# First gate's small operations on GpSimd, results in the place of low parts, a third bank for first products and a fifth split in the last segment

## The chip, the cores and the metric

The kernel runs on one core of a Trainium2 chip. Five engines work side by side, each on its own stream of instructions, and semaphores order them: TensorE (PE, matrix products), VectorE (DVE), ScalarE (ACT), GpSimd (POOL) and SyncE (SP, which issues transfers). The metric is the device time of one execution in microseconds. Three executions of the kernel before took 925.42, 928.76 and 929.61 us; the median is 928.76.

## The reference

Three stages, all in float32:

```python
# 1. attention within hash buckets: 2 batches, 8 heads, 768 positions, 64 dimensions, 6 sign bits
mask = q_bucket[:, :, :, None] == k_bucket[:, :, None, :]
scores = where(mask, q @ k.T / 8, -1e9);  attn = softmax(scores);  x = attn @ v   # -> 1536 x 512
# 2. mixture of 8 experts, noisy top 2
logits = x @ w_gate;  scale = log1p(exp(x @ w_noise));  noisy = logits + scale * noise
# the two largest of 8 per token, weights softmaxed over the two
for e in experts: out[tokens of e] += weight * (relu(x @ w1[e]) @ w2[e])           # 512 -> 1024 -> 512
# 3. second layer
h = x @ w_in;  out = (h - tanh(h)) @ w_out                                         # 512 -> 2048 -> 512
```

The inputs of the third stage come in float64 and are turned into float32 on the chip (`convert`).

## The kernel before, in words

*Products.* Every float32 operand is split into a high part (a copy in the format that PE takes at full rate) and a low part (the rest, a subtraction). A product is three PE passes: high by high, low by high, high by low. For weights, `split_w` makes both parts: ScalarE copies the high part (L851), then a subtraction makes the low part (L850): on GpSimd in two halves for the experts 0, 1 and 7, on DVE otherwise. Each weight tile holds two 128 x 512 blocks, one of the first matrix and one of the second. `fetch` brings the raw tile from memory into a buffer `wraw` of the pool `stg`, which has two of them; `next_w` fetches if needed and splits the next weight.

*Attention.* There are 16 heads in a row (2 batches of 8), 12 steps ("frames") a head, written out by hand in `plan`: `at_frame(t, f)` starts a generator at frame t, and each `yield` in it leaves the rest to the next frame. PE, DVE, ScalarE and SP take their instructions in this order. Per frame PE computes a block of scores for the row maximum (`smax`, L414, two banks of PSUM; DVE reduces it, L415) and a block for the exponential (`st_unit`, ScalarE L450, into one of five tiles p) and adds up p by v (`pv`). The sums of p over six blocks are five adds a head (`psum`, L483), on GpSimd or, where a bit of `PSV` is set, on DVE. GpSimd also has `vsum`, `nmterm`, the add in `evac` (L529) and the scatters.

*Gate.* Batch 0 is complete halfway through the heads, and its gate (`gate(0)`) runs beside the attention of batch 1, from frame 140 on: exponential on ScalarE, logarithm by three Newton steps, noise, top 2 by DVE's maximum and index search, one-hot `oh`, matrix `M`, prefix sums by PE (L709), positions `sidx`. The 128 tokens of a column of x then go by an indirect transfer on GpSimd's queue (`scatter`, L742) to their expert's rows in `Xg`. `gate(1)` runs after the attention, on DVE, with the first products of segment 0 as fill work for PE (`seg_fine`, `fill`): PE's order there is written by hand (`FILL`), and 30 of the 32 pieces stand before the first transposes of segment 1, whose rows `load_x(1)` reads from `Xg` once the scatters have landed. `gate_w` computes the two weights of each token, `results` the rows to gather later.

*Experts.* There are ten segments: expert 0 and expert 7 in two of 240 rows, one for each batch, the others with 448 rows. A segment has eight steps; a step is a first product (`h_step`, bank "b"), relu and its low part, and a second product (`y_step`, banks "c" and "d"). `y_out` copies the results from PSUM to SBUF, for the short segments into a `wraw` buffer, and `store` writes them to `Y`. `trans_x` transposes the next segment's rows (L1061) and makes their parts `xh` and `xl`. `LASTV` and `LASTW` list the steps of the last two segments in which another weight is split. At step 1 of segment 1 comes a branch (`overflow`) that all engines take part in.

*Second layer.* Four blocks of 384 rows with 16 steps each. `h2_step` computes the first product (bank "b", two banks), then tanh and a polynomial on ScalarE, DVE (L1379, L1381, L1383; the last of them frees the bank) and GpSimd (L1374), and the hidden rows' parts (L1394, L1399); `o2_step` the second product; `combine` transposes the rows of the next block, through bank "a".

Of the kernel before, what the change touches and what calls it, by code (L numbers as in the profile page):

```python
# [33 lines left out]
PSV = (0, 32, 32, 32, 32, 32, 32, 32, 32, 0, 0, 32, 0, 60, 32, 44)  # L34
# [9 lines left out]
LASTW = (2, 3, 5, 7)  # L44
# [32 lines left out]
def body(tc, q, k, v, proj, w_gate, w_noise, noise, w1, w2, w_in, w_out, out):  # L77
# [22 lines left out]
    with ExitStack() as ctx:  # L100
# [464 lines left out]
        def tables():  # L565
# [5 lines left out]
            nc.vector.tensor_tensor(spl, ends[:, 0], ends[:, 1], op=ALU.add)  # L571
            yield
            nc.vector.tensor_scalar(capv, spl, float(SEG - CAP), float(CAP), op0=ALU.mult, op1=ALU.add)
            b0 = basev[:, 0]
            nc.vector.tensor_scalar(b0, io8, float(CAP), float(B * SEG - CAP), op0=ALU.mult, op1=ALU.add)
# [45 lines left out]
        def gate(b):  # L621
            w = lambda name, shape, dt=F32: gx.tile(shape, dt, name=name)
            early = b < B - 1
            l3 = gd["lg", b].rearrange("p (c e) -> p c e", c=NC)
            y = w("g_y", [128, NC, E])
            nc.scalar.activation(y, l3[:, :, E:2 * E], AF.Exp)
            u = w("g_u", [128, NC, E])
            nc.vector.tensor_scalar(u, y, 1.0, None, op0=ALU.add)
            ln = w("g_ln", [128, NC, E])
            if b == B - 1:  # L630
                nc.scalar.activation(ln, u, AF.Ln)
            else:


                yield
                nc.vector.tensor_scalar(ln, u.bitcast(I32), LN2 * 2.0 ** -23, 0.0298 - 127 * LN2, op0=ALU.mult, op1=ALU.add)
                yield

            r = w("g_r", [128, NC, E])
            nc.vector.scalar_tensor_tensor(r, u, -1.0, y, op0=ALU.add, op1=ALU.subtract)  # L640
            if early:
                yield
            rc = w("g_rc", [128, NC, E])
            nc.vector.reciprocal(rc, u)
            if early:
                yield
            nc.vector.tensor_tensor(r, r, rc, op=ALU.mult)
            if early:
                yield
            nc.vector.tensor_tensor(r, r, nz[:, b], op=ALU.mult)  # L650
            if early:
                yield
            nc.vector.tensor_tensor(r, l3[:, :, 0:E], r, op=ALU.subtract)
            yield
            ei = w("g_ei", [128, NC, E])
            for _ in range(3 if b < B - 1 else 0):
# [6 lines left out]
                yield  # L663
                nc.vector.scalar_tensor_tensor(ln, ue, -1.0, ln, op0=ALU.add, op1=ALU.add)
                yield
            ny = w("g_ny", [128, NC, E])
            nc.vector.tensor_tensor(ny, ln, nz[:, b], op=ALU.mult)
            if early:
                yield
            nc.vector.tensor_tensor(ny, ny, r, op=ALU.add)  # L670
            yield
            v8 = w(f"g_v8{b}", [128, NC, 8])
            i8 = w("g_i8", [128, NC, 8], U32)
            for c in range(NC):
                nc.vector.max(out=v8[:, c], in_=ny[:, c])
# [8 lines left out]
            nc.vector.tensor_copy(e12, i8[:, :, 0:2].rearrange("p c t -> p t c"))  # L684
            yield
# [3 lines left out]
            if early:  # L689
# [3 lines left out]
                                    io8[:, None, None, :].to_broadcast([128, 2, NC, E]), op=ALU.is_equal)  # L693
            if early:
                yield
            nc.vector.tensor_tensor(M[:, b], oh[:, 0], oh[:, 1], op=ALU.add)
            yield
            if early:
                yield
# [20 lines left out]
            if early:  # L720
# [3 lines left out]
            else:  # L724
                pick(sidx[:, :, b], oh, ts)

        def pick(*a_):
            for _ in pick_steps(*a_):
                pass
# [800 lines left out]
```

## Time and profile before

| | us |
|---|---|
| median of three runs | 928.76 |
| the profiled execution: its own time | 933.93 |
| its span, first to last instruction | 932.1 |
| PE busy | 897.7 (96%) |
| DVE busy | 677.7 (73%) |
| ScalarE busy | 539.9 (58%) |
| GpSimd busy | 372.8 (40%) |

The profile is of one execution. Busy times are unions of an engine's instructions; an engine that isn't the slowest may stand idle at no cost. The idle time in front of an instruction is put down to what ended it. In the rows below, "L415" is line 415 of the kernel, and a tile's name stands without its buffer number.

### The profile page before, as it was taken

The page shows a single profiled execution, that of the slowest core. Times are in us where ns is not written, and L with a number is a line of the kernel's source. Part 1 is how long each engine was busy: PE and PEld are TensorE (multiplying, and loading weights), DVE is VectorE, ACT ScalarE, POOL GpSimd, SP SyncE. Part 2 cuts the span into 40 slices and gives each one's busy share as a digit, 9 for nine tenths or more (in the row PEclk, how much of TensorE's full clock was granted, in tenths as well). Part 3 has the DMA queues.
Part 4 walks back from the last instruction along what each step waited for, and adds up shares of the span by engine and source line. Part 5 has one row for each costly group of instructions (what it writes and reads, how often), then busy time and mean ns, then how long its engine had stood idle before and what let it go on. Part 6 is the DMA issues. An engine that isn't in the chain of part 4 may idle for free.

```text
span 932.1 us, 13632 instructions
## 1 busy us (share of the span) xinstructions
PE 897.7 (96%) x4736; PEld 699.3 (75%) x4736; DVE 677.7 (73%) x1290; ACT 539.9 (58%) x1039; POOL 372.8 (40%) x325
## 2 busy tenths in 40 slices
PE   8999999998997788999999999999999999999998
PEld 3555555554556677888888888888889899989997
DVE  7788787889757325797887878665888677677665
ACT  7658666864453133444444444454777777777765
POOL 6687778875667443000000004602342342342221
PEclk9999999999999899999999999999999999999999
DMA  5635553300222478686858777555420110110000
GB/s 123 171 117 170 159 182 106 103 24 7 93 64 95 163 222 256 218 287 214 271 199 292 236 255 248 174 197 179 135 69 1 57 46 1 57 46 1 35 1 34
DMA packets 104625, 123.72 MB, mean 133 GB/s; under 512 B 32121, under 2 KB 75177, under 8 KB 104553
## 3 DMA queue, kind: packets, MB, share of 16 engines
q1 hardware_dynamic: 100712, 110.23, 37.6%
q0 software_dynamic: 3840, 12.59, 4.0%
q8 instruction: 38, 0.62, 0.3%
q14 instruction: 35, 0.28, 0.1%
HBM read 82.79 MB, written 37.72 MB: 129 GB/s over the span
## 4 chain that ended last, share of the span: by engine, by line
PE 55%; DVE 3%; ACT 1%; DMA 1%; issue 1%; POOL 0%; DVEq 0%; SPq 0%; POOLq 0%
PE bank L1068 9%; PE bank L1070 9%; PE bank L1069 9%; PE bank L1095 8%; PE bank L1094 8%; PE bank L1093 8%; PE bank L1110 2%; PE bank L1061 1%; DVE g_u L1381 1%; PE bank L1350 1%; DMA xy<-Xg 1%; DVE wt L850 1%; DMA Y<-xy 0%; DVE hh L1399 0%; DVE g_u L1383 0%
## 5 line engine op out<-in xcount | busy, mean ns | idle before, releaser
L1068 PE MATMUL bank<-xh,wt 128*128 128x384 f32 (+2 forms) x544 | 186.3, 342 | 4.8 <-DVE g_u L1383 2.8
L1069 PE MATMUL bank<-xl,wt 128*128 128x384 f32 (+2 forms) x544 | 183.1, 337 | 0.0
L1070 PE MATMUL bank<-xh,wt 128*128 128x384 f32 (+2 forms) x544 | 183.1, 337 | 0.0
L1093 PE MATMUL bank<-wt,hh 128*128 128x512 f32 (+1 forms) x400 | 159.6, 399 | 9.5 <-ACT hh L1084 6.1
L850 POOL TENSOR_TENSOR wt<-wraw,wt 128x512 fp32r<-128x512 f32 x48 | 68.5, 1451 | 246.8 <-ACT wt L851 234.7
L1095 PE MATMUL bank<-wt,hh 128*128 128x512 f32 (+1 forms) x400 | 159.3, 398 | 0.1
L1094 PE MATMUL bank<-wt,hh 128*128 128x512 f32 (+1 forms) x400 | 158.9, 397 | 0.0
L1374 POOL TENSOR_TENSOR g_th<-g_h,g_th 128x384 f32<-128x384 f32 x64 | 67.2, 1050 | 187.2 <-ACT g_th L1373 186.7
L450 ACT ACTIVATE p<-bank 128x384 f32<-128x384 f32 x192 | 91.8, 489 | 72.1 <-PE bank L449 66.1
L415 DVE TENSOR_REDUCE mx<-bank 128x1 f32<-128x384 f32 x192 | 103.3, 551 | 31.1 <-PE bank L414 29.0
L1068 PEld LDWEIGHTS bank<-xh,wt 128*128 128x128 f32 x544 | 102.5, 188 | 13.9 <-DVE g_u L1383 4.8
L1069 PEld LDWEIGHTS bank<-xl,wt 128*128 128x128 f32 x544 | 102.5, 188 | 6.7 <-DVE xl L1353 0.2
L851 ACT ACTIVATE wt<-wraw 128x1024 fp32r<-128x1024 f32 x80 | 84.2, 1054 | 36.4 <-PE bank L1110 20.5
L1070 PEld LDWEIGHTS bank<-xh,wt 128*128 128x128 f32 x544 | 102.4, 188 | 3.1
L1093 PEld LDWEIGHTS bank<-wt,hh 128*128 128x128 f32 (+1 forms) x400 | 75.6, 189 | 22.9 <-ACT hh L1084 6.4
L483 POOL TENSOR_TENSOR ps<-ps,p 128x768 f32<-128x768 f32 x47 | 85.9, 1827 | 11.7 <-ACT p L450 7.1
L1095 PEld LDWEIGHTS bank<-wt,hh 128*128 128x128 f32 (+1 forms) x400 | 75.5, 189 | 18.3 <-DVE hh L1399 0.6
L1084 ACT ACTIVATE hh<-bank 128x448 fp32r<-128x448 f32 (+1 forms) x80 | 37.7, 473 | 83.6 <-PE bank L1070 34.9
L1086 DVE SCALAR_TENSOR_TENSOR hh<-bank,hh 128x384 fp32r<-128x384 f32 (+2 forms) x128 | 45.8, 388 | 54.7 <-ACT hh L1084 46.0
L1094 PEld LDWEIGHTS bank<-wt,hh 128*128 128x128 f32 (+1 forms) x400 | 75.5, 189 | 12.8
L474 PE MATMUL bank<-p,v 128*64 128x384 f32 x384 | 83.8, 515 | 0.0
L448 PE MATMUL bank<-qc,kb 108*128 108x384 f32 (+1 forms) x192 | 79.2, 412 | 1.8 <-DVE qc L438 1.6
(250 smaller groups left out, 1629.4 us busy)
## 6 DMA issues: line engine op xcount, KB each, us to landing
wraw<-in_moe_w_dram SPq DMA_DIRECT2D x128, 256.0 KB
cv_t<-in_moe_w_in_dram SPq DMA_DIRECT2D x16, 512.0 KB
cv_t<-in_moe_w_out_dram SPq DMA_DIRECT2D x16, 512.0 KB
W2f<-cv_w SPq DMA_DIRECT2D x16, 512.0 KB
wraw<-W2f SPq DMA_DIRECT2D x16, 512.0 KB
Xg<-zero SPq DMA_DIRECT2D x14, 512.0 KB
Y<-zero SPq DMA_DIRECT2D x9, 512.0 KB
xy<-Xg SPq DMA_DIRECT2D x6, 768.0 KB
```

The costliest lines, as they stand in the source:

```text
L415: nc.vector.tensor_reduce(MX[i % 2][:, c, hf:hf + 1], ps[:, :HF], op=ALU.max, axis=AX.X)
L448: nc.tensor.matmul(ps[:, :HF], KB[sn(g, par)][r, ck(kc)], QC[sn(g, par)][r, half(hf)], start=True, stop=False)
L450: nc.scalar.activation(hd["p", i, kc][:, half(hf)], ps[:, :HF], AF.Exp, scale=float(D) ** -0.5)
L474: nc.tensor.matmul(hd["o", i][hf * D:(hf + 1) * D, :HF], raw["v", g][:, par, kc], hd["p", i, kc][:, half(hf)], start=(kc == 0), stop=(kc = ...
L483: eng.tensor_tensor(t, hd["p", i, 0] if kc == 1 else t, hd["p", i, kc], op=ALU.add)
L851: nc.scalar.activation(t[:, 0], r, AF.Copy)
L1068: nc.tensor.matmul(ps[:, :n], ws(0, dc), xh[:, dc, :n], start=(dc == 0), stop=False)
L1069: nc.tensor.matmul(ps[:, :n], ws(0, dc), xl[:, dc, :n], start=False, stop=False)
L1070: nc.tensor.matmul(ps[:, :n], ws(1, dc), xh[:, dc, :n], start=False, stop=(dc == KD4 - 1))
L1093: nc.tensor.matmul(ps[:m], a, t[:, 0, 1], start=first, stop=False)
L1094: nc.tensor.matmul(ps[:m], a, t[:, 1, 1], start=False, stop=False)
L1095: nc.tensor.matmul(ps[:m], l, t[:, 0, 1], start=False, stop=last)
```

## The change

- `gate(0)` and `gate_w(0)`: sums, products, casts and copies move from DVE to GpSimd (`eng`); an operation that DVE does in one instruction with two steps becomes two on GpSimd. Reciprocals, maxima, index search, one-hot and everything that reads PSUM stay on DVE. At each hand-over the generator yields three more frames (`lead`). Both index columns are picked at once; the second half had been picked after attention. Head 10's last add of p moves from GpSimd to DVE (`PSV`). Three operations of `tables` move to GpSimd.
- The low parts of the two weights split beside `gate(1)` are kept back (`hd["lows"]`) until the gate's last step and are then made on DVE, in front of the scatters.
- `y_out` of short segments writes into the low-part tile `xl` of its own segment's rows, not into a `wraw` buffer.
- In the last segment a fifth weight is split (`LASTW`), and from its step 3 two raw weights may be fetched ahead. The transposes for the last segment come a step later.
- In the first block of the second layer, first products turn over three banks, until the next block's rows are transposed; until then "a" has one bank.

```diff
-PSV = (0, 32, 32, 32, 32, 32, 32, 32, 32, 0, 0, 32, 0, 60, 32, 44)
+PSV = (0, 32, 32, 32, 32, 32, 32, 32, 32, 0, 32, 32, 32, 60, 32, 44)
-LASTW = (2, 3, 5, 7)
+LASTW = (2, 3, 5, 6, 7)
...
         def gate(b):
...
+            eng = nc.gpsimd if early else nc.vector
+            lead = range(3 if early else 0)
...
+            eng.tensor_scalar(u, y, 1.0, None, op0=ALU.add)
...
+            if early:
+                eng.tensor_scalar(ln, u.bitcast(I32), LN2 * 2.0 ** -23, 0.0298 - 127 * LN2, op0=ALU.mult, op1=ALU.add)
...
+                eng.tensor_scalar(r, u, -1.0, None, op0=ALU.add)
+                eng.tensor_tensor(r, r, y, op=ALU.subtract)
+            for _ in lead:
+                yield
...
             nc.vector.reciprocal(rc, u)
...
+            eng.tensor_tensor(r, r, rc, op=ALU.mult)
+            eng.tensor_tensor(r, r, nz[:, b], op=ALU.mult)
+            eng.tensor_tensor(r, l3[:, :, 0:E], r, op=ALU.subtract)
...
+            for n in range(3 if early else 0):
+                if n:
+                    nc.scalar.activation(ei, ln, AF.Exp, scale=-0.5)
+                    yield
                 ue = w("g_ue", [128, NC, E])
-                nc.vector.tensor_tensor(ue, u, ei, op=ALU.mult)
-                yield
-                nc.vector.tensor_tensor(ue, ue, ei, op=ALU.mult)
-                yield
-                nc.vector.scalar_tensor_tensor(ln, ue, -1.0, ln, op0=ALU.add, op1=ALU.add)
-                yield
+                eng.tensor_tensor(ue, u, ei, op=ALU.mult)
+                eng.tensor_tensor(ue, ue, ei, op=ALU.mult)
+                eng.tensor_scalar(ue, ue, -1.0, None, op0=ALU.add)
+                eng.tensor_tensor(ln, ln, ue, op=ALU.add)
+                if n < 2:
+                    for _ in lead:
+                        yield
...
+            eng.tensor_copy(e12, i8[:, :, 0:2].rearrange("p c t -> p t c"))
...
+            eng.tensor_tensor(M[:, b], oh[:, 0], oh[:, 1], op=ALU.add)
...
-                gd["rest"] = (sidx[:, 1:2, b], oh[:, 1:2], ts)
-                yield from pick_steps(sidx[:, 0:1, b], oh[:, 0:1], ts)
+            for _ in pick(sidx[:, :, b], oh, ts, eng, lead):
+                yield
...
             nc.scalar.activation(t[:, 0], r, AF.Copy)
-            if key in (0, 1, E - 1):
+            if "lows" in hd:
+                hd["lows"].append(lambda: low(nc.vector, slice(0, 2)))
+            elif key in (0, 1, E - 1):
...
             if nb == 2:
-                yo = stg.tile([128, 2, DM], F32, name="wraw")
+                yo = mx[n % 2].tile([128, KD4, CAP], F32, name="xl")
+                yo = yo.rearrange("p c n -> p (c n)")[:, 0:2 * DM].rearrange("p (j d) -> p j d", j=2)
...
-        pick(*gd["rest"])
         run(scatter, 0, 1)
...
+        hd["lows"] = []
         next_w()
         gen = gate(B - 1)
...
+        for fn_ in hd.pop("lows"):
+            fn_()
         run(scatter, B - 1, 0)
         load_x(1)
...
-                while fn[0] < min(wn[0] + (PF if "st" in rings else 1), len(wsrc)):
+                while fn[0] < min(wn[0] + (PF if "st" in rings else 2 if last and f >= 3 else 1), len(wsrc)):
...
-                    if f == (5 + dc // 2 if n == B - 1 else 3 + dc):
+                    if f == (5 + dc // 2 if n == B - 1 else min(4 + dc, 6) if n == NSG - 2 else 3 + dc):
                         trans_x(n + 1, dc)
...
+        banks.update(a=[1], b=[2, 3, 0])
+        nbank["b"] %= 2
...
                 if f == 11 + j:
+                    if t0 == BC:
+                        banks.update(a=[0, 1], b=[2, 3])
+                        nbank.update(a=0, b=min(nbank["b"] % 3, 1))
                     combine(t0)
```

## Rows read from the trace of the kernel before

**Rows 1.** Windows by heads: length; busy us of each engine (instructions); PE clock; DMA

```profile
69.60:179.30 109.70, 109.70 (x643) 63.09 (x643) 88.07 (x188) 80.17 (x170) 85.67 (x71) 1.00 0.49 150
179.30:196.80 17.50, 17.40 (x103) 9.43 (x99) 14.48 (x34) 9.98 (x21) 14.92 (x12) 1.00 0.22 54
196.80:213.70 16.90, 16.19 (x93) 9.18 (x94) 16.31 (x36) 13.25 (x31) 12.64 (x13) 1.00 0.00 1
213.70:233.60 19.90, 16.92 (x92) 8.78 (x92) 19.61 (x54) 8.54 (x18) 10.75 (x7) 0.94 0.04 9
233.60:249.60 16.00, 15.79 (x81) 9.14 (x81) 11.53 (x30) 7.45 (x16) 11.37 (x9) 0.96 0.17 66
```

**Rows 2.** PE's waits over the span: us in total, times, longest

```profile
PE bank L1068 <- DVE g_u L1383: 2.8, 5, 1.0
...
PE bank L414 <- DVE mx L415: 1.8, 3, 1.4
```

**Rows 3.** Groups on DVE, 190 to 258 us: busy us, mean ns | idle before

```profile
L483 DVE TENSOR_TENSOR ps<-ps,p 128x768 f32<-128x768 f32 x5 | 4.7, 950 | 0.1
L662 DVE TENSOR_TENSOR g_ue<-g_ue,g_ei 128x48 f32<-128x48 f32 x3 | 4.0, 1322 | 0.0
...
L781 DVE TENSOR_TENSOR wAB<-g_f 128x6 f32<-128x6 f32 x1 | 0.8, 796 | 0.0
...
L628 DVE TENSOR_SCALAR g_u<-g_y 128x48 f32<-128x48 f32 x1 | 0.7, 657 | 0.1
...
L667 DVE TENSOR_TENSOR g_ny<-g_ln,nz 128x48 f32<-128x48 f32 x1 | 0.2, 199 | 0.0
```

**Rows 4.** Groups on GpSimd over the span

```profile
L483 POOL TENSOR_TENSOR ps<-ps,p 128x768 f32<-128x768 f32 x47 | 85.9, 1827 | 11.7 <-ACT p L450 7.1 <-DVE ps L483 2.2
...
L457 POOL TENSOR_TENSOR vs<-vs,v 128x128 f32<-128x128 f32 x32 | 14.6, 458 | 2.2
```

**Rows 5.** Timeline behind attention, several engines: start us, us, engine line; [idle before <- releaser]

```profile
293.18 4.96 POOL L850 TENSOR_TENSOR wt<-wraw,wt 128x512 fp32r<-128x512 f32 x4
...
294.40 3.78 DVE L684 CAST g_e<-g_i 128x12 f32<-128x12 uint32 x1 [0.71 <-DVE g_i L680]
...
299.05 0.20 PE L709 MATMUL bank<-M,before 128*128 128x48 bf16 x1 [4.31 <-DVE M L696]
...
301.19 0.99 POOL L742 DMA_INDIRECT Xg<-x,sidx  x1 [3.04 <-DVE tots L794]
...
310.38 0.41 SPq L1048 DMA_DIRECT2D xy<-Xg  x1
...
318.89 0.78 PE L1093 MATMUL bank<-wt,hh 128*120 128x512 f32 x1 [5.14 <-ACT hh L1084]
```

**Rows 6.** Timeline at the start of expert 1

```profile
356.35 0.52 ACT L1084 ACTIVATE hh<-bank 128x448 fp32r<-128x448 f32 x1
...
359.05 0.69 DVE L1125 COPY wraw<-bank 120x512 f32<-120x512 f32 x1 [1.45 <-POOL wt L850]
...
359.88 0.47 PE L1093 MATMUL bank<-wt,hh 128*128 128x512 f32 x1 [2.80 <-DVE wraw L1125]
```

**Rows 7.** Window behind that wait, columns as in rows 1

```profile
359.80:365.00 5.20, 5.12 (x16) 4.25 (x17) 4.25 (x6) 3.18 (x4) 3.27 (x2) 0.67 0.76 196
```

**Rows 8.** Timeline: the last segment's rows, issue and first use

```profile
612.77 0.35 SPq L1048 DMA_DIRECT2D xy<-Xg  x1
...
617.97 0.40 PE L1061 MATMUL bank<-ident,xy 120*128 120x120 f32 x2 [0.50 <-DMA xy<-Xg]
```

**Rows 9.** Timeline: the fifth wait for a bank, second layer

```profile
689.41 0.44 PE L1068 MATMUL bank<-xh,wt 128*128 128x384 f32 x1 [0.45 <-DVE g_u L1383]
```

**Rows 10.** Timeline: a scatter's issue beside DVE's add, and a low part on DVE

```profile
246.51 0.96 DVE L483 TENSOR_TENSOR ps<-ps,p 128x768 f32<-128x768 f32 x1
...
246.64 1.68 POOL L742 DMA_INDIRECT Xg<-x,sidx  x1 [0.17 <-issue]
...
365.96 1.21 DVE L850 TENSOR_TENSOR wt<-wraw,wt 128x1024 fp32r<-128x1024 f32 x1
```

More of the change, by code (lines that the diff above doesn't have):

```diff
@@ L570, in tables @@
             yield
-            nc.vector.tensor_tensor(spl, ends[:, 0], ends[:, 1], op=ALU.add)
+            nc.gpsimd.tensor_tensor(spl, ends[:, 0], ends[:, 1], op=ALU.add)
             yield
-            nc.vector.tensor_scalar(capv, spl, float(SEG - CAP), float(CAP), op0=ALU.mult, op1=ALU.add)
+            nc.gpsimd.tensor_scalar(capv, spl, float(SEG - CAP), float(CAP), op0=ALU.mult, op1=ALU.add)
             b0 = basev[:, 0]
-            nc.vector.tensor_scalar(b0, io8, float(CAP), float(B * SEG - CAP), op0=ALU.mult, op1=ALU.add)
+            nc.gpsimd.tensor_scalar(b0, io8, float(CAP), float(B * SEG - CAP), op0=ALU.mult, op1=ALU.add)
             yield
@@ L674, in gate @@
             for c in range(NC):
+                if early and c == NC // 2:
+                    yield
                 nc.vector.max(out=v8[:, c], in_=ny[:, c])
@@ L683, in gate @@
             e12 = w(f"g_e12{b}", [128, 2, NC])
-            nc.vector.tensor_copy(e12, i8[:, :, 0:2].rearrange("p c t -> p t c"))
-            yield
+            eng.tensor_copy(e12, i8[:, :, 0:2].rearrange("p c t -> p t c"))
+            if not early:
+                yield
+            else:
+                for _ in lead:
+                    yield
             AB = w("g_AB", [128, 2, NC])
@@ L692, in gate @@
             nc.vector.tensor_tensor(oh, AB[:, :, :, None].to_broadcast([128, 2, NC, E]),
-                                    io8[:, None, None, :].to_broadcast([128, 2, NC, E]), op=ALU.is_equal)
+                              io8[:, None, None, :].to_broadcast([128, 2, NC, E]), op=ALU.is_equal)
             if early:
                 yield
-            nc.vector.tensor_tensor(M[:, b], oh[:, 0], oh[:, 1], op=ALU.add)
+            eng.tensor_tensor(M[:, b], oh[:, 0], oh[:, 1], op=ALU.add)
             yield
-            if early:
+            for _ in lead:
                 yield
@@ L755, in gate_w @@
             v8, e12 = gd[b][3:]
+            early = b < B - 1
+            eng = nc.gpsimd if early else nc.vector
+            lead = range(3 if early else 0)
             dlt = w("g_d", [128, NC])
-            nc.vector.tensor_tensor(dlt, v8[:, :, 1], v8[:, :, 0], op=ALU.subtract)
+            eng.tensor_tensor(dlt, v8[:, :, 1], v8[:, :, 0], op=ALU.subtract)
+            for _ in lead:
+                yield
             nc.scalar.activation(dlt, dlt, AF.Exp)
-            if b < B - 1:
+            if early:
                 yield
@@ L762, in gate_w @@
             sm = w("g_sm", [128, NC])
-            nc.vector.tensor_scalar(sm, dlt, 1.0, 1e-9, op0=ALU.add, op1=ALU.add)
+            eng.tensor_scalar(sm, dlt, 1.0, 1e-9, op0=ALU.add, op1=ALU.add)
             yield
+            for _ in lead:
+                yield
             nc.vector.reciprocal(ws[:, 0], sm)
-            nc.vector.tensor_tensor(ws[:, 1], ws[:, 0], dlt, op=ALU.mult)
-            if b < B - 1:
+            if early:
                 yield
+            eng.tensor_tensor(ws[:, 1], ws[:, 0], dlt, op=ALU.mult)
             f = w("g_f", [128, 2, NC])
@@ L831, in results @@
                 yield
-                pick(yidx[:, :, b], oh, ty)
+                run(pick, yidx[:, :, b], oh, ty)
                 yield
```

83 lines of the change are left out of this document (34 added, 49 removed).

## Prediction

> **What bounds the kernel now.** I read the page's busy shares first: TensorE (PE) is busy for 96% of the span, so only the stretches where it stands, or where work comes to it slowly, can give time. The 40 slices show three such stretches, 190 to 250 us, 280 to 372 us and 605 to 700 us, and the two ends. I then asked for the stretches by window, for PE's idle rows, and for what the engine named there was doing.
>
> (a) Attention with the first gate beside it, 179 to 250 us. Seven heads at steady pace take 109.70 us, 15.67 each; the next four take 17.5, 16.9, 19.9 and 16.0, together 70.3, which is 7.6 more than 4 x 15.67 [rows 1]. In the third, VectorE (DVE) is busy for 19.61 of 19.90 us. The longest of PE's three waits for a row maximum on DVE is 1.4 us [rows 2]. The gate's operations make DVE late: one on 48 columns takes 0.20 us undisturbed, but the three of L662 took 1.32 on average, with GpSimd's 1.83 us adds beside them [rows 3, 4].
>
> (b) The second gate, after attention. GpSimd subtracts four low parts in 4.96 us from 293.18; DVE's cast of 12 columns, started at 294.40, takes 3.78 and ends with them, and PE stands 4.31 us until the gate's matrix M is there [rows 5].
>
> (c) The start of expert 1: PE stands 2.80 us for the copy of the segment's results, and that copy waited for GpSimd's low part, because results and raw weights share two buffers [rows 6]. The granted clock is 0.67 in the 5.2 us behind it [rows 7].
>
> (d) The last segment and the first steps of the second MoE: 0.50 us for the rows of the last segment [rows 8], and five waits on DVE's L1383, 2.8 us in all [rows 2], which means that the next first product has no bank. The last of them is 0.45 us [rows 9].
>
> **The change, part by part.** *First gate on GpSimd.* Thirty DVE operations between 191.55 and 256.6, 16.0 us by their own rows, leave DVE (first L628 0.66, last L781 0.80, thirty in all [rows 3]); 22 of them, 13.7 us, lie in the four heads. DVE's busy time there is 14.48 + 16.31 + 19.61 + 11.53 = 61.9 us [rows 1]; less 13.7, plus one 0.95 us add of head 10 that comes to DVE [rows 3], it is 49.2 in 62.7 us, 78%, against 80% at steady pace (88.07 of 109.70). So DVE stops being late. GpSimd gets 27 operations there and 8 behind, since it does a fused one as two. Their price is not in the trace on GpSimd: its add of 128 columns takes 0.458 us and of 768 columns 1.827 [rows 4], 2.14 ns a column, so 48 columns take 0.29 at the lower end and 0.46 at the upper; I take 0.36, nearer the lower since there are 48 columns. 27 x 0.36 = 9.7 us, less one add of 1.83: 49.7 becomes 57.6 of 62.7 us, 92%. That is more than its 78% at steady pace, and GpSimd takes work in order: behind a gate operation that waits for DVE or ScalarE stand the sums of p, which hold the five p buffers. So I take 4.5 of the 7.6 us; the ends are 7.6 and a loss, the rival below. The gate's 3-step spacing hides the hand-overs as long as GpSimd is under 4 us late. The rest of the old pick (second halves of the indices) leaves DVE at attention's end; PE's transposes end just before it, so nothing is taken for it, nor for the three table operations.
>
> *Low parts of two weights kept back.* With GpSimd's four subtractions gone from 293 us, the cast takes some 0.2 us like the gate's other small ones, M comes 3.6 us earlier and PE has its fill work until 294.8. The indices and scatters could then start 3.6 to 4.2 us earlier. But both subtractions now stand on DVE directly before the scatters, 2 x 1.21 us [rows 10], and a scatter issue on GpSimd took 1.68 us with a DVE add of two SBUF operands beside it, 0.99 elsewhere [rows 5, 10]. So the first scatter may lose up to 2.4 us. The load of the next segment is issued at 310.38 [rows 5]; such a load took 5.2 us to its use in the last segment (612.77 to 617.97 [rows 8]), so its rows are there at 315.6. PE without its unexplained 5.14 us wait would want them at about 315.2 (318.89 - 5.14 + 1.4 for one second product at full clock). Both move; the later one, the load, sets the gain: 1.8 to 4.2, I take 2.3. The low parts are wanted only at the eighth product and in the next segment, so their lateness is hidden by the fill; DVE's other low parts come up to 2.4 us later, which PE's slack before the load covers.
> The Trainium skill, page "SBUF — State Buffer", section "Who interferes with whom", has it that a tensor_tensor takes only the read interface shared with GpSimd, while descriptor generation needs the write one, and marks this as inferred. The 1.68 us row speaks against it; by the rule this part would give 4.2 us.
> The 5.14 us wait stays as it is in the sum: its row names ScalarE, but nothing on ScalarE explains it.
>
> *Results in the place of low parts.* The copy no longer waits for a weight's buffer: PE goes on at 357.1 in place of 359.88. What is late next are the first hidden rows of expert 1: ScalarE's relu starts at 356.35 and takes 0.52, then comes DVE's low part, some 0.7 like its copy of 512 columns [rows 6], so 357.6 for the block's third product, and PE waits up to 0.5. The low clock costs 0.33 x 5.2 = 1.7 us [rows 7] and goes with the wait. 2.8 + 1.7 - 0.5 = 4.0; lower end 1.0 (the weights' landing replaces the buffer), upper 4.5. The store reads the low-part buffer until it lands; the next writer of that buffer comes more than ten us later, so no new wait. With the buffers free, the weights' transfers start earlier too; I take nothing.
>
> *Third bank, fifth split, later transposes.* With three banks the first product waits for the step before; what is late next is the low part of the hidden rows (L1399), behind L1383 in DVE's order, for which the second product waits; of 0.45 us a step [rows 9] I take it to give 0.3 once, not in each, since DVE's pace is unchanged. DVE sets the pace in the five steps with a split (1.21 us of it on DVE [rows 10]); taken out of the fifth, it ends that a step sooner: the last wait, 0.45, and a lag of about 0.25 behind it, 0.7. In the last segment the split adds its 1.21 us on DVE ahead of the last block's transposed low part: 0.3 lost. The later transposes win the 0.50 us wait [rows 8] and give 0.2 back, since two now stand directly before the product that needs them. Together 1.0; the ends are -1.2 (the split in PE's way) and 3.3 (every wait gone).
>
> **Sum.** 4.5 + 2.3 + 4.0 + 1.0 = 11.8 us. The profiled execution took 933.93 us (span 932.1), so it would be 922.1; the runs' median of 928.76 is 5.2 lower, and less 11.8 it is **917.0 us**.
>
> **Rivals.**
> *GpSimd becomes the bound.* For: 92% at my price, and at 0.46 an operation 60.3 of 62.7 us before any wait for the lock. Against: head 13 gives it one add in place of four. The first term is then nothing: 917 + 4.5 = 921.5. The Trainium skill, "GPSIMD Engine Reference", section "4.1 Engine selection", is against elementwise work there too, with VectorE about twice as fast; the 1.83 us add beside DVE's 0.95 [rows 3, 4] agrees, and by twice 0.20 us an operation takes 0.40.
> *The weights' landing replaces the buffer* at expert 1: ScalarE's split ahead of the relu is fed by a transfer, and the queue is busy there (DMA share 0.76 [rows 7]). The third term is 1.0: 920.
> *The lows don't hold the scatters* (the page's rule above): the second term is 4.2, 915.1.
> *The gains are not kept:* the load of the second segment and the branch behind it are paced by transfers, so (a) and (b) come back as a wait there; only (c) and (d) stay, at half: 926.3.
> *Slower: GpSimd stands at the gate's hand-overs.* Seven times the gate goes from GpSimd to ScalarE or DVE and back. If GpSimd stands about 4 us each, with p's sums queued behind it, it needs 57.6 + 28 = 85.6 us where it had 70.3: 15.3 longer in place of 4.5 shorter, 917 + 4.5 + 15.3 = 936.8. It decides from 20 us of standing (57.6 + 12.7 + 7.3). For: GpSimd is in order. Against: the three steps kept free at each hand-over, about 4 us.
>
> **How the numbers follow.** Forecast 0.46, GpSimd the bound 0.15, weights 0.12, lows without effect 0.10, gains not kept 0.10, slower 0.07. About 0.5%, 4.6 us, is what a measurement of this kernel can tell from no change. Faster by more (under 924.1): 0.46 + 0.10 + most of 0.15 and 0.12, 0.81; within: 0.12; slower 0.07. The range runs from all upper ends together (7.6 + 4.2 + 4.5 + 3.3 = 19.6, so 909) to 926, nearly the case of gains not kept.
>
> **What would show it.** Right: the four heads at 16.5 us or less each and no L660 to L670 on DVE there; the cast behind the index search at 0.2 us and no 4.31 us wait; scatter issues stretched beside two DVE subtractions; no wait above 0.6 us at expert 1's first second-product and a full clock there; waits on L1383 gone, shorter ones on L1399 in their place. Wrong: GpSimd over 95% busy beside heads of 17 us and more; first products waiting for ScalarE's exponentials; a wait of several us for the second segment's rows.

## The result, and the profile after

The changed kernel took 915.24 us (median of four, 914.14 to 916.18), the kernel before 929.13 beside it (925.42 to 929.61). The ratio is 0.9855, with a 95% interval of 0.983 to 0.988: 13.5 us faster. I had said 917.0. A later session gave less: 919.14 (914.98 to 919.58) against 925.62, ratio 0.9906 (0.988 to 0.9932), 8.7 us. The ratios here and below go by all runs and are not quotients of the two medians, which would give 0.9930 and 6.5 us there. The sum came out close, in part by luck: its first term is not there on average, and the other three are together 3.2 us larger than I had said, as the rest of this text shows.

In the kernel after, lines have moved: first products are L1085 to L1087 (before L1068 to L1070), second products L1110 to L1112 (L1093 to L1095), the second segment's transposes L1078 (L1061), the low part of a weight L865 (L850), its high part L866 (L851), scatters L752 (L742), the gate's cast L694 (L684), the two last operations of the second layer's first products L1405 (L1383) and L1416/L1421 (L1394/L1399).

From the page of the changed kernel, its span, its busy times, and PE's row of 40 slices (each digit tenths):

```profile
span 912.1 us, 13613 instructions
PE 890.4 (98%) x4736; PEld 696.3 (76%) x4736; DVE 660.7 (72%) x1257; ACT 540.5 (59%) x1039; POOL 374.7 (41%) x357
...
PE   8999999999989899999999999999999999999998
```

PE went from 96% to 98%: of PE's busy time 7 us went, mostly half-clock stretches, and of its idle time 13. PE's waits after, largest first (line waited at, what ended it, us in total, times, longest):

```profile
PE bank L1078 <- DMA xy<-Xg: 3.5, 1, 3.5
PE bank L490 <- DVE ps L483: 3.0, 2, 2.4
PE bank L535 <- POOL x L529: 2.3, 1, 2.3
PE bank L1110 <- ACT hh L1416: 1.2, 4, 0.3
```

None of the waits that the prediction set out from [rows 2, 5, 6] is there any more; three new ones stand ahead. The heads of the first gate, in windows bounded like those of [rows 1] (length, then busy time of PE, its weight loads, DVE, ScalarE, GpSimd, then the granted clock, DMA share and GB/s):

```profile
179.00:196.10 17.10, 17.10 (x105) 9.37 (x99) 12.48 (x31) 9.85 (x21) 14.35 (x15) 1.00 0.23 56
196.10:213.90 17.80, 15.48 (x95) 8.93 (x93) 12.78 (x29) 13.27 (x30) 16.43 (x29) 1.00 0.00 1
213.90:230.00 16.10, 15.72 (x90) 8.77 (x87) 14.21 (x49) 8.43 (x18) 10.86 (x10) 1.00 0.06 11
230.00:245.10 15.10, 14.98 (x87) 8.73 (x86) 11.52 (x27) 7.67 (x17) 10.80 (x13) 1.00 0.13 52
245.10:259.40 14.30, 13.96 (x78) 7.39 (x78) 10.16 (x27) 7.27 (x16) 11.72 (x13) 1.00 0.77 256
259.40:273.60 14.20, 11.84 (x71) 6.64 (x70) 5.41 (x12) 7.74 (x19) 13.66 (x15) 1.00 0.11 37
```

The first four rows are the four heads of the sum, heads 10 to 13; they hold the same PE instructions as before and take 66.1 us in place of 70.3. In the second row GpSimd is busy for 16.43 of 17.80 us, and PE stands 2.3. The last row is head 15, where PE stands 2.4 us and GpSimd is busy for 13.66 of 14.20.

To compare more than one pair, I cut every profile at the same PE instructions: I from head 10's start to the end of attention (179.5 to 274.2 us before), II the second gate up to the first transpose of segment 1 (to 321.6), III the branch and the start of expert 1 (to 367.2), IV the last segment and the first steps of the second layer (610.6 to 700.0). The kernels are those of the next section; in brackets the time for which the granted clock was one half. The remaining stretches differ by at most 1.6 us between all kernels.

| kernel (profiled execution) | I | II | III | IV |
|---|---|---|---|---|
| before | 94.71 (3.4) | 47.39 (8.3) | 45.60 (5.4) | 89.35 |
| gate_alone | 93.95 (3.2) | 38.43 (0.9) | 44.38 (6.1) | 89.62 |
| lows_alone | 93.91 (0) | 37.49 (0) | 42.77 (3.4) | 89.98 |
| results_alone | 95.76 (6.8) | 40.76 (3.4) | 38.20 (0) | 89.75 |
| end_alone | 94.95 (3.4) | 41.11 (6.8) | 41.79 (3.4) | 88.35 |
| index_whole | 94.01 (0) | 40.80 (4.8) | 46.31 (5.5) | 89.69 |
| changed kernel | 92.46 (0) | 37.88 (1.3) | 39.45 (5.5) | 87.50 |
| after_again | 96.83 (10.1) | 38.89 (1.3) | 39.43 (5.6) | 87.50 |
| no_lows | 97.65 (10.2) | 42.22 (5.2) | 37.80 (1.6) | 87.45 |
| gatew_vec | 100.29 (13.7) | 38.93 (2.2) | 38.58 (1.2) | 88.12 |
| lows_late | 98.92 (13.7) | 38.53 (1.4) | 40.36 (5.4) | 87.72 |
| res0_raw | 93.98 (3.4) | 37.04 (0) | 41.01 (3.4) | 88.02 |
| no_bank | 96.75 (10.2) | 38.83 (0) | 38.45 (3.4) | 88.12 |
| best | 94.38 (6.8) | 37.98 (0) | 38.58 (3.4) | 87.74 |

### The profile page after: what moved, and what is told of

It is laid out like the page before. It is cut to its first block, busy times and chain, and to the rows that moved or that the text cites. A ratio compares the mean times of both kernels' runs of the same rounds, so it can differ in the third digit from the quotient of the medians.

```text
span 912.1 us, 13613 instructions
## 1 busy us (share of the span) xinstructions
PE 890.4 (98%) x4736; PEld 696.3 (76%) x4736; DVE 660.7 (72%) x1257; ACT 540.5 (59%) x1039; POOL 374.7 (41%) x357
## 4 chain that ended last, share of the span: by engine, by line
PE 61%; DVE 2%; ACT 1%; issue 0%; POOL 0%; DVEq 0%
PE bank L1085 10%; PE bank L1086 10%; PE bank L1087 10%; PE bank L1112 9%; PE bank L1111 9%; PE bank L1110 9%; PE bank L1127 2%; PE bank L1078 1%; DVE g_u L1403 1%; PE bank L1372 1%; DVE wt L865 0%; DVE g_u L1415 0%; DVE hh L1421 0%; DVE g_u L1405 0%; ACT hh L1416 0%
## 5 line engine op out<-in xcount | busy, mean ns | idle before, releaser
L1085 PE MATMUL bank<-xh,wt 128*128 128x384 f32 (+2 forms) x544 | 185.8, 342 | 0.1
L1087 PE MATMUL bank<-xh,wt 128*128 128x384 f32 (+2 forms) x544 | 183.3, 337 | 0.0
L865 POOL TENSOR_TENSOR wt<-wraw,wt 128x512 fp32r<-128x512 f32 x44 | 63.8, 1469 | 234.5 <-ACT wt L866 228.2
L1110 PE MATMUL bank<-wt,hh 128*128 128x512 f32 (+1 forms) x400 | 158.7, 397 | 1.2 <-ACT hh L1416 1.2
L1112 PE MATMUL bank<-wt,hh 128*128 128x512 f32 (+1 forms) x400 | 158.8, 397 | 0.7 <-DVE hh L1103 0.5
L1085 PEld LDWEIGHTS bank<-xh,wt 128*128 128x128 f32 x544 | 102.7, 189 | 7.2 <-ACTq L1279 0.6
L1087 PEld LDWEIGHTS bank<-xh,wt 128*128 128x128 f32 x544 | 102.5, 188 | 3.1
L866 ACT ACTIVATE wt<-wraw 128x1024 fp32r<-128x1024 f32 x80 | 84.3, 1055 | 24.5 <-PE bank L1127 20.4
L1112 PEld LDWEIGHTS bank<-wt,hh 128*128 128x128 f32 (+1 forms) x400 | 74.9, 187 | 19.7 <-DVE hh L1421 1.7
L1110 PEld LDWEIGHTS bank<-wt,hh 128*128 128x128 f32 (+1 forms) x400 | 75.0, 188 | 14.7 <-ACT hh L1416 2.4
L483 POOL TENSOR_TENSOR ps<-ps,p 128x768 f32<-128x768 f32 x45 | 82.3, 1828 | 4.9 <-DVE ps L483 2.2
L865 DVE TENSOR_TENSOR wt<-wraw,wt 128x1024 fp32r<-128x1024 f32 (+1 forms) x62 | 71.2, 1150 | 9.6 <-ACT wt L866 9.6
```

The costliest lines, as they stand in the source:

```text
L483: eng.tensor_tensor(t, hd["p", i, 0] if kc == 1 else t, hd["p", i, kc], op=ALU.add)
L865: low = lambda eng, h: eng.tensor_tensor(t[:, 1, h], r[:, h], t[:, 0, h].bitcast(F32), op=ALU.subtract)
L866: nc.scalar.activation(t[:, 0], r, AF.Copy)
L1085: nc.tensor.matmul(ps[:, :n], ws(0, dc), xh[:, dc, :n], start=(dc == 0), stop=False)
L1087: nc.tensor.matmul(ps[:, :n], ws(1, dc), xh[:, dc, :n], start=False, stop=(dc == KD4 - 1))
L1110: nc.tensor.matmul(ps[:m], a, t[:, 0, 1], start=first, stop=False)
```

## The experiments

Three sessions of four kernels, each session on another chip and beside the kernel before; no_bank ran only once.

| kernel | us | before | ratio, 95% interval |
|---|---|---|---|
| gate_alone | 923.73 | 927.81 | 0.9950, 0.9931 to 0.9970 |
| lows_alone | 922.83 | 927.81 | 0.9956, 0.9942 to 0.9970 |
| results_alone | 920.83 | 927.81 | 0.9927, 0.9907 to 0.9947 |
| end_alone | 925.30 | 927.81 | 0.9977, 0.9961 to 0.9994 |
| index_whole | 933.95 | 934.43 | 1.0000, 0.9981 to 1.0019 |
| no_lows | 921.76 | 934.43 | 0.9863, 0.9846 to 0.9881 |
| gatew_vec | 923.56 | 934.43 | 0.9888, 0.9869 to 0.9908 |
| lows_late | 921.86 | 934.43 | 0.9857, 0.9839 to 0.9875 |
| after_again | 919.14 | 925.62 | 0.9906, 0.9880 to 0.9932 |
| best | 915.39 | 925.62 | 0.9879, 0.9856 to 0.9903 |
| res0_raw | 918.50 | 925.62 | 0.9921, 0.9893 to 0.9950 |
| no_bank | 919.28 (one run) | 925.62 | none |

### Each part alone

The four parts of the diff, each put on the kernel before by itself.

> The kernel before with the first part alone: first gate's sums and products on GpSimd, with the three table operations, PSV[10] = 32 and the whole index pick in place of its two halves. Theory 1 (read from the two traces): the four heads win 4.7 us and head 15 gives 2.4 back, because the last weights' six small operations stand on GpSimd ahead of the sums of p; 2.3 to 2.5 us in all, so about 926.7 against 929.1. Theory 2 (my prediction's term): the 2.4 us lost in head 15 belong to the other parts, the gate alone is worth 4.5: 924.6. The trace decides by PE's wait at L490 in head 15.

> The kernel before with the second part alone: the low parts of two weights kept back past the second gate and taken on VectorE. Theory 1: it moves the matrix M, the scatters and the load of the second segment 4 us earlier and wins 2.7 us, 926.4; the 3 us that the changed kernel wins behind the branch (PE's 2.0 us there, 1.1 us at the next second product) are not here. Theory 2: these 3 us come with it, since everything is issued earlier: 5.7 us, 923.4. Prediction's term: 2.3.

> The kernel before with the third part alone: results of the four two-block segments written to the place of the low parts. Theory 1: the buffers of raw weights come free, so their transfers start before the second segment in place of behind its predecessor's store; the branch wait and the 1.1 us wait behind it go too: 4.65 + 3.0 = 7.7 us, 921.4. Theory 2: only the copy at the start of expert 1 is freed and the clock behind it: 4.65 us, 924.5 (prediction's term: 4.0, 925.1).

> The kernel before with the fourth part alone: third bank, fifth split, later transposes. Theory 1: 1.85 us, as the two traces differ behind 610 us: 927.3. Theory 2 (prediction's term): 1.0 us, 928.1. Nothing before 600 us is changed here, so its trace also shows again what the kernel before does at 318.89 us: if the 5.14 us wait there belonged to the one profiled execution alone, this trace has none over 1 us before that second product; if it belongs to the kernel, it is there again.

By the ratios they gain 4.6, 4.1, 6.8 and 2.1 us: 17.6 together, more than the 13.5 of the whole. Two of the parts must buy the same thing, and the traces say which. In gate_alone the low parts are still on GpSimd, and yet PE's wait for M, 4.31 us before [rows 5], is 1.2. Two of PE's waits in gate_alone (lines are those of each kernel; M's are L723 and L710 here):

```profile
PE bank L490 <- DVE ps L483: 3.0, 2, 2.4
...
PE bank L723 <- DVE M L710: 1.2, 1, 1.2
```

And the order of time there, GpSimd's rows from 287 us and DVE's cast (start, duration, line):

```profile
287.61 2.53 POOL L865 TENSOR_TENSOR wt<-wraw,wt 128x512 fp32r<-128x512 f32 x2 [2.81 <-ACT wt L866]
291.56 2.58 POOL L865 TENSOR_TENSOR wt<-wraw,wt 128x512 fp32r<-128x512 f32 x2 [1.42 <-ACT wt L866]
...
294.34 0.17 DVE L694 CAST g_e<-g_i 128x12 f32<-128x12 uint32 x1
```

The four low parts start at 287.61 and 291.56, not all at 293.18 [rows 5], and are over when the cast comes. In the kernel before six scatter issues stood ahead of them, those of the index half that was picked after attention. The order of time in the kernel before, first and last of the six:

```profile
285.77 1.01 POOL L742 DMA_INDIRECT Xg<-x,sidx  x1 [0.16 <-DVE x L527]
...
292.21 0.98 POOL L742 DMA_INDIRECT Xg<-x,sidx  x1 [0.30 <-issue]
```

With both halves picked at once these six move to 248 to 256 us, beside head 14. So theory 1 for gate_alone was right about head 15 (L490, 2.4 us) and missed this; theory 2's gain, 4.5 us, is near the measured one for another reason than it gave. lows_alone lies between its theories (4.1 us, 2.8 to 5.4); the wait for M is gone, and the wraw wait at expert 1 still there (2.0). results_alone went by theory 1: 6.8 us (4.9 to 8.6), where theory 1 said 7.7 and theory 2 4.65. end_alone's interval (0.6 to 3.6 us) holds both theories; in stretch IV it is 88.35 against a mean of 89.68 in the five profiles without this part, 1.3 us. It and results_alone leave the work from 300 to 320 us as it was, and PE stands for no more than 1.2 us there: the 5.14 us of [rows 5] don't belong to every execution (last section).

### The scatters alone, and the change without the low parts

```diff
# index_whole, on the kernel before
-                gd["rest"] = (sidx[:, 1:2, b], oh[:, 1:2], ts)
-                yield from pick_steps(sidx[:, 0:1, b], oh[:, 0:1], ts)
+                yield from pick_steps(sidx[:, :, b], oh, ts)
...
-        pick(*gd["rest"])
# no_lows, on the changed kernel: split_w, and the lines that open and empty the list
-            if "lows" in hd:
-                hd["lows"].append(lambda: low(nc.vector, slice(0, 2)))
-            elif key in (0, 1, E - 1):
+            if key in (0, 1, E - 1):
```

> The kernel before with one thing changed: both halves of the first gate's indices are taken at once, where the first half stood, and the second half at the end of attention is gone. Gate, adds and low parts stay where they were. Theory 1: in the kernel before six second scatters stand on GpSimd from 285.77 to 293.2 us, ahead of the four low parts; with the indices known early they are issued earlier, the low parts come earlier, and the 12-column cast and PE's 4.31 us wait go to about 1.2 us, as they did with the gate alone: 3 us faster, 924.8 against 927.8. Theory 2: the cast's wait is the low parts' own and goes only when they leave GpSimd: no change, 927.8, or slower by the larger index operations in head 13.

> The changed kernel without the lows kept back (they are on GpSimd again). Theory 1: the early scatters have already freed GpSimd, so PE's wait for M is 1.2 us in place of none, and the first scatter issue is 0.98 in place of 1.77 us: 0.4 us slower than the changed kernel, 915.6. Theory 2: the lows kept back are worth here what they were worth alone on the kernel before, 5.0 us: 920.2. My prediction's term for them: 2.3, 917.5.

PE's waits in index_whole, before the second product and for M:

```profile
PE bank L1092 <- issue: 4.3, 1, 4.3
...
PE bank L709 <- DVE M L696: 1.2, 1, 1.2
```

The cast there:

```profile
294.49 0.17 DVE L684 CAST g_e<-g_i 128x12 f32<-128x12 uint32 x1
```

At its place theory 1 holds to the digit: two lines of index code, with the gate still on DVE, take the cast to 0.17 us and the wait from 4.31 to 1.2. The time did not follow (933.95 against 934.43, 1.8 us to either side); its profile is of its fastest execution (927.84 of 927.84 to 938.73) and so can't say where the 3.1 us went in the others. That stays open; the last section names a loss in head 14, beside these scatters, that other kernels of the second session had and this profile has not. no_lows: 0.9863 beside 0.9857 for lows_late, the changed kernel with an edit without effect (below), in the same session. So the low parts kept back are worth 0.6 us with the scatters early, by intervals of 1.6 us to either side each: theory 1's 0.4 fits, the 5.0 that they bring alone does not. In stretch II no_lows does take 3.3 to 3.7 us more than gatew_vec and lows_late, but 2.1 of that is a longer standstill of the kind in the last section (5.5 us against 3.4) and 1.2 the wait for M, and its stretch III is shorter. What they cost shows in GpSimd's rows of no_lows:

```profile
295.41 2.58 POOL L865 TENSOR_TENSOR wt<-wraw,wt 128x512 fp32r<-128x512 f32 x2 [1.42 <-ACT wt L866]
301.37 1.01 POOL L752 DMA_INDIRECT Xg<-x,sidx  x1 [3.38 <-DVE tots L809]
```

Its first scatter issue takes 1.01 us where the changed kernel's takes 1.77 (next part).

### The lows behind the scatters

```diff
-        for fn_ in hd.pop("lows"):
-            fn_()
         run(scatter, B - 1, 0)
         load_x(1)
+        for fn_ in hd.pop("lows"):
+            fn_()
```

> The changed kernel with the two kept-back low parts taken behind the first six scatters and the load of the second segment, in place of ahead of them. Theory 1 (the row of the changed kernel): two subtractions on VectorE, 2.36 us from 293.89, hold the first scatter issue at 1.77 in place of 0.98 us; it comes back to 1.0, the scatters and the load are 0.8 us earlier, PE's 3.5 us wait for the load is 2.7: 0.8 us faster, 914.4. Theory 2 (the Trainium skill, page SBUF - State Buffer, section Who interferes with whom: a tensor_tensor leaves descriptor generation alone): the first issue stays at 1.7 us and the time at 915.2.

The edit moved nothing: DVE takes the two subtractions in its own order, right behind the indices, whatever GpSimd's program says. Its rows are those of the changed kernel, 6.9 us later. So it told nothing apart: with the subtractions still beside it, the first issue takes its 1.77 us by either theory. The changed kernel in order of time, DVE, GpSimd, SP's load and PE's first transpose of those rows:

```profile
291.06 0.17 DVE L694 CAST g_e<-g_i 128x12 f32<-128x12 uint32 x1
...
293.89 1.22 DVE L865 TENSOR_TENSOR wt<-wraw,wt 128x1024 fp32r<-128x1024 f32 x1
...
294.24 1.77 POOL L752 DMA_INDIRECT Xg<-x,sidx  x1 [11.10 <-DVE sidx L748]
296.31 0.98 POOL L752 DMA_INDIRECT Xg<-x,sidx  x1 [0.30 <-issue]
...
304.62 0.41 SPq L1065 DMA_DIRECT2D xy<-Xg  x1
...
309.61 0.63 PE L1078 MATMUL bank<-ident,xy 120*128 120x120 f32 x2 [3.46 <-DMA xy<-Xg]
```

What does tell it apart is the set of all 14 profiles: the first issue took 1.73 to 1.77 us in the eight with two such subtractions on DVE beside it, 0.99 to 1.01 in the six without. Page "SBUF — State Buffer" of the Trainium skill, section "Who interferes with whom", has it that a tensor_tensor leaves descriptor generation alone, an inference by its own words; here it does not. The price is 0.8 us, not the 2.4 of my bound: one issue is held for about as long as the first subtraction still had to run, 0.87 us; the next issue takes 0.98.

### The weight step of the first gate on VectorE

```diff
             early = b < B - 1
-            eng = nc.gpsimd if early else nc.vector
+            eng = nc.vector
```

> The changed kernel with the first gate's weight step (the nine small sums and products behind the indices) on VectorE again, the gate itself left on GpSimd. Theory 1: the 2.36 us for which PE stands at L490 in head 15 come from the six small operations and the hand-overs ahead of the sums of p on GpSimd; the wait goes: 2.4 us faster, 912.8. Theory 2: GpSimd is late there by its twelve scatter issues from 240 to 256 us, and the wait stays above 1.5 us: 914.5 or more.

The wait at L490 went (0.8 us in two, the longest 0.6), but so did it in lows_late and no_lows, in the same session, without this edit: there head 14 took 20.0 and 20.1 us, where it takes 14.0 in the changed kernel. Head 14 in no_lows and in the changed kernel:

```profile
247.30:267.40 20.10, 17.41 (x79) 8.44 (x79) 10.41 (x25) 6.87 (x15) 17.01 (x21) 0.83 0.57 195
...
245.40:259.40 14.00, 13.96 (x78) 7.39 (x78) 9.86 (x25) 6.98 (x15) 11.59 (x12) 1.00 0.78 261
```

PE stood in no_lows and lows_late three times for 0.8 to 0.95 us beside the scatters and then ran at half clock for 6.8 us, and GpSimd was no longer late. gatew_vec lost as much in that head (21.6 us). Its ratio, 0.9888, is the worst of the three, with intervals that overlap. Theory 1 is not shown: in the second session PE came too late to wait for GpSimd.

### Where the results go

```diff
             if nb == 2:
-                yo = mx[n % 2].tile([128, KD4, CAP], F32, name="xl")
...
+                if n == 0:
+                    yo = stg.tile([128, 2, DM], F32, name="wraw")
+                else:
+                    yo = mx[n % 2].tile([128, KD4, CAP], F32, name="xl")
```

> The changed kernel with the results of the first segment alone back in a buffer of raw weights, those of the second segment and of the last two still in the place of low parts. Theory 1: the transfers of the next weights wait for that segment's store again, PE's branch wait (2.0 us in the kernel before) and the 1.1 us at the second product behind it come back, and the start of expert 1 stays without its 2.8 us wait: 2 to 3 us slower than the changed kernel. Theory 2 (my prediction, which took nothing for earlier transfers): the whole gain hangs on the second segment's results, and this kernel takes as long as the changed one.

SP's rows and ScalarE's split in res0_raw:

```profile
306.07 0.39 SPq L893 DMA_DIRECT2D wraw<-in_moe_w_dram  x1
314.75 0.35 SPq L1148 DMA_DIRECT2D Y<-wraw  x1
315.15 1.74 SPq L895 DMA_DIRECT2D wraw<-in_moe_w_dram  x1
...
320.60 1.06 ACT L866 ACTIVATE wt<-wraw 128x1024 fp32r<-128x1024 f32 x1 [4.87 <-DMA wraw<-in_moe_w_dram]
```

The second half of a raw weight (L895) is issued at 315.15, behind the first segment's store; ScalarE then stands 4.87 us for it with the branch behind it, and PE at the branch, by its waits:

```profile
PE bank L1085 <- ACTq L1282: 2.5, 1, 2.5
```

The changed kernel's rows for the same:

```profile
295.60 0.51 SPq L895 DMA_DIRECT2D wraw<-in_moe_w_dram  x1
...
296.73 0.68 SPq L895 DMA_DIRECT2D wraw<-in_moe_w_dram  x1
...
318.75 1.06 ACT L866 ACTIVATE wt<-wraw 128x1024 fp32r<-128x1024 f32 x1 [1.03 <-PE bank L1112]
```

Two whole weights are fetched by 297 us, and ScalarE waits for PE, not for a transfer. Stretch III is 41.01 against a mean of 38.86 in the eight profiles with all results in the low parts' place: 2.2 us, theory 1 by its mechanism. What it is worth in all is less clear: stretch II is the shortest of all there (37.04), and over II and III together res0_raw takes 78.1 us where the changed kernel, after_again, no_bank and best take 76.6 to 78.3, 77.4 on average. By time the two kernels can't be told apart (0.9921 and 0.9906).

### The third bank

no_bank leaves out the two `banks.update` pieces of the change and keeps the fifth split and the later transposes.

> The changed kernel without the third bank for first products, the fifth split and the later transposes kept. Read from its trace between 610 and 700 us of the kernel before, where the changed kernel won 1.7 + 0.2 us. Theory 1 (prediction: 0.3 for the bank, 0.7 for the split): the five waits for VectorE's L1403, 2.8 us in all in the kernel before, are four or five again, and about 0.3 us is lost. Theory 2: the bank carries nearly all of it, since the first of these waits is 1.0 us: 1.3 us lost.

Four of the five waits for DVE are back (at L1405, which is L1383 before; the L1403 of the expectation is a slip), but stretch IV is 88.12 against a mean of 87.72 in the seven profiles with the whole part (87.45 to 88.12): 0.4 us, no more than those differ among themselves. That is theory 1, the prediction's 0.3, and not theory 2; with the bank, waits of 1.2 us on L1416 stand in the place of these 2.3. PE's wait in no_bank:

```profile
PE bank L1085 <- DVE g_u L1405: 2.3, 4, 1.0
```

### The changed kernel again, and a better one

best is the changed kernel with four edits: the two of the parts before (weight step, lows), and

```diff
-... 32, 32, 32, 60, 32, 44)
+... 32, 32, 32, 60, 48, 44)
...
-            (nc.vector if i >= NI - 1 else nc.gpsimd).tensor_tensor(xs, xs, hd["t", i], op=ALU.add)
+            (nc.vector if i >= NI - 1 or i == 9 else nc.gpsimd).tensor_tensor(xs, xs, hd["t", i], op=ALU.add)
```

> The changed kernel once more, on the chip of the three runs beside it, as their base. Its ratio was 0.9855 (0.983 to 0.988). Theory: its two waits in attention (2.3 us at L535, 2.4 at L490) and the 3.5 us before the second segment are there again; the half-clock stretches may lie elsewhere, since in ten profiles they followed all eleven PE waits of over 3 us, but only eight of fourteen between 2 and 3. Rival: the waits themselves differ from chip to chip, and then a comparison of single traces tells little.

> The changed kernel with GpSimd relieved at the two places where PE waited for it: the x add of head 9 on VectorE (2.3 us wait at L535), one more sum of head 14 on VectorE (PSV[14] = 48) and the weight step of the first gate on VectorE (2.4 us at L490); and the kept-back low parts behind the first six scatters (0.8). Theory 1: the three waits go to 0.9, 0 and 2.7: 4.6 us faster than the changed kernel, ratio to before 0.9805. Theory 2: VectorE becomes late in heads 11 to 14 as it was before the change, waits for row maxima come back, and nothing is left: 0.9855.

after_again has the first profile's waits in attention again, by PE's waits:

```profile
PE bank L490 <- DVE ps L483: 3.0, 2, 2.4
PE bank L535 <- POOL x L529: 2.3, 1, 2.3
```

And yet stretch I is 4.4 us longer and II 1.0. Windows of after_again at and behind those two waits (columns as in [rows 1]; behind GpSimd the granted clock, the DMA share and GB/s):

```profile
204.00:208.00 4.00, 1.68 (x14) 0.95 (x10) 1.40 (x4) 2.27 (x7) 3.67 (x8) 1.00 0.00 0
208.10:211.30 3.20, 3.20 (x13) 2.19 (x10) 0.96 (x3) 0.62 (x3) 2.79 (x7) 0.50 0.00 0
...
269.60:276.20 6.60, 6.17 (x24) 3.64 (x25) 1.10 (x3) 1.82 (x6) 5.29 (x4) 0.50 0.25 78
```

Here the clock went to 1.2 GHz (0.50 in the row) behind both waits, for 3.4 and 6.8 us, with PE busy; in the first profile it did so behind neither. PE's list of waits in attention is otherwise the same.

best: 914.97 to 915.47 in five runs, after_again 914.98 to 919.58 in six. The medians differ by 3.75 us, but the intervals of the ratios overlap: probably better, not shown to be. The waits at L535 and L490 are gone (0.6 left of the latter), and a new one is there:

```profile
PE bank L434 <- DVE nm L428: 3.5, 2, 3.3
```

DVE's rows ahead of it, and one of GpSimd's beside them:

```profile
253.54 1.73 DVE L788 TENSOR_TENSOR g_f<-g_e 128x6 f32<-128x6 f32 x1
...
256.10 1.82 POOL L483 TENSOR_TENSOR ps<-p 128x768 f32<-128x768 f32 x1
256.20 1.75 DVE L792 TENSOR_TENSOR wAB<-g_t 128x6 f32<-128x6 f32 x1
...
258.13 1.70 DVE L796 TENSOR_TENSOR wAB<-g_f 128x6 f32<-128x6 f32 x1
```

Three DVE operations on six columns, 0.16 us each elsewhere, take 1.7: two beside GpSimd's adds of p, the first beside the end of a scatter issue and an add of 384 columns; the row maxima behind them are late and PE stands 3.3 us. The weight step should have stayed on GpSimd, where it took 0.21 us an operation. best without that edit was not tried.

## Why the prediction came out, step by step

**First gate on GpSimd (4.5 us).** The prices held: GpSimd's sums and products of 48 columns took 0.28 to 0.33 us each and started 0.36 to 0.41 apart where one reads the other's result (0.36 taken); DVE is busy for 51.0 of the 66.1 us (77%; I had 78%). In the first profile the four heads won 4.2 us. GpSimd was far less full than I said, 52.4 of 66.1 us in place of 57.6 of 62.7, and yet it was late twice: in the second of the four heads four gate operations stand ahead of an x add (L529; PE 2.3 us at L535), in head 15 six of the weight step and the adds behind the twelve scatters stand ahead of the last sum (2.4 us at L490). The first wait goes when that add leaves GpSimd (best); the second went in best too, which takes both the weight step and a sum away, so which of the two makes it is not shown. The step that failed is "The gate's 3-step spacing hides the hand-overs": it keeps the gate from waiting, not what is queued behind the gate. The relief of DVE itself was there: at the same PE instructions the four heads take 70.4 us on average in the five profiles with the gate on DVE (69.6 to 71.5), 67.7 in eight with it on GpSimd (66.2 to 69.1), and 64.4 in best, without the wait at L535. But the end of the stretch, with head 15, took 2.4 to 5.2 us longer in the five profiles with the wait at L490. Over seven profiles of kernels with the gate and its weight step on GpSimd, stretch I takes 95.8 us on average, over five without 94.7: nothing of the 4.5 is left. In two of the seven (no_lows, lows_late) it is not GpSimd's queue but the 6 us in head 14, for which no row names a cause; the other five average 94.8, and that too leaves nothing. What this part really brought stands in a sentence of mine that took nothing for it: "The rest of the old pick ... leaves DVE at attention's end". With it went six scatters from GpSimd, and 3.1 of the 4.31 us wait.

**Low parts kept back (2.3 us).** Right as a mechanism and at its place: the cast takes 0.17 us, the wait is gone, the first scatter issue is stretched, and the load then sets the end: issued 304.62, used 309.61, 5.0 us (I took 5.2), with PE standing 3.46 us. I had named a wait of several us for these rows as a sign against me; it is what limits the term, as its sum said. Stretch II is 41.4 us in the three profiles with neither this nor the early scatters (before less its 5.14), 37.5 with the low parts alone, 38.4 with gate_alone, 38.1 with both (five profiles; those of the second session are left out, since all four have the standstill of the last section in this stretch): 3.2 us, bought by either and not twice. So this term and the first shared one gain.

**Results in the place of low parts (4.0 us).** Too small: 5.3 us by stretch III (five profiles 44.2, eight 38.9). At expert 1 the 2.80 us wait went, with no 0.5 us left and no half clock behind it, 4.65 between the first two profiles; the changed kernel's window there, to be laid beside [rows 7]:

```profile
343.00:348.30 5.30, 5.30 (x26) 4.65 (x26) 5.23 (x7) 2.13 (x3) 3.82 (x2) 1.00 0.93 253
```

PE is busy for all of it at full clock. What I took nothing for, the weights' earlier transfers, has its part in the 5.3: 2.2 us by res0_raw's stretch III, 0.7 by its II and III together. That leaves 3.1 to 4.6 us for the freed copy and the clock behind it, near the 4.0 I had said; the term was too small by what it left out.

**Third bank, fifth split, later transposes (1.0 us).** The waits of [rows 8, 9] are gone, and 2.0 us by stretch IV: the bank 0.4 (0.3 said), the others 1.6 (0.7 said). Which of the two is larger was not tried.

The sum by stretches is -1.1 + 3.2 + 5.3 + 2.0 = 9.4 us (10.4 without the two profiles that lost 6 us in head 14), between the sessions' 8.7 and 13.5. The prediction's 11.8 lies there because errors cancel: the first term is 4.5 too high or more, the other three are 3.2 too low together. The sum is luck in that; the mechanisms of the last three held at their places. Rivals: GpSimd as the bound is half true (late, not full); the weights' landing did not replace the buffer; the slower case did not come, since GpSimd was late behind the gate, not in it; the scatters were held, but by 0.8 us; and PE's wait for the load came back with 3.5 us, but did not take all of the gain behind attention.

## What to carry to other kernels

When an operation leaves a late place, list what it releases on other engines' queues: here six transfers issued 40 us earlier took 3.1 us from one of PE's waits, while the 30 operations moved brought nothing on average; index_whole, which has the transfers alone, shows that gain in its trace but not in its time. Spacing a chain of hand-overs protects the chain; what is queued behind it on an in-order engine needs its own check. Price a PE wait with the clock that may follow it, and judge parts of a few us by several profiles, cut at the same instructions.

## What the runs showed of the hardware

- Half clock behind waits. In the 14 profiles, all 15 PE waits of over 3 us were followed within 2 us, or already overlapped, by a stretch at 1.2 GHz, and 14 of 22 between 2 and 3 us, each mostly 3.4 or 6.8 us long. The same kernel had 10.1 us of it in stretch I in one execution and none in another, for 4.4 us.
- A wait without a cause in any row. In five of the 14 profiles (before, and the four of the second session) PE stood 3.3 to 5.5 us before the second product near 310 us; the rows name ScalarE's hidden rows or PE's own issue. In all five PE goes on 0.4 us after ScalarE's relu starts, and that relu is what is late: ScalarE had stood for 7.4 to 8.2 us, PE's last product had ended 2.9 to 5.1 us before, and what released ScalarE is not in the trace ("remote"). Scatters were being issued, or had just been, each time. The relu of the kernel before, behind [rows 5]:

```profile
318.47 0.63 ACT L1084 ACTIVATE hh<-bank 128x240 fp32r<-128x240 f32 x2 [8.21 <-remote]
```

The loss in head 14 of no_lows, lows_late and gatew_vec (20.0 to 21.6 us in place of 14.0) also lies beside scatter issues, in the same session. Whether it is the same thing is not shown. In that session the kernel before took 934.43 us, in the others 929.13, 927.81 and 925.62. The cause of both stays open.
